# Y blocks loaded once into raw buffers, and the sums of the weight blocks spread over three conversion steps

## The chip, the cores and the metric

The kernel runs on one core of one Trainium2 chip. TensorE (PE) multiplies, VectorE (DVE), ScalarE (ACT) and GpSimd (POOL) do the elementwise work, and SyncE (SP) issues nearly all transfers. Each engine works through its own queue in order. The metric is device time in microseconds for one launch, the median of several runs.

## What is computed

Nystrom attention, its output as 2304 tokens of 512 features, and two MLPs behind each other. What the change touches lies in the second MLP.

```python
x = attn_out.transpose(0, 2, 1, 3).reshape(2304, 512)
h = x @ w_in            # 512 -> 2048
x = (h - np.tanh(h)) @ w_out
h = x @ w2_in           # second MLP
return (h * np.tanh(softplus(h))) @ w2_out
```

The matrices arrive as 64-bit floats, and are converted to 32-bit floats on the chip, from the two 32-bit halves of each number.

## The kernel before

**First MLP.** It runs in 128 slots (32 per batch entry, 16 per half of its tokens, one for each 128 hidden features). A slot multiplies (`h1`, L599 to L601), evicts and applies the function (`vec`: ACT, DVE, and POOL up to slot 103; L637 is DVE's last read of the product), and adds the product of three slots before into y (`y1`). At the end of 16 slots y goes through a raw buffer into DRAM (`ys`).

**Second MLP.** The tokens come in three blocks of 768 (`u`), the hidden features in eight blocks of 256 (`j`); one (u, j) is a group, `k` = 0 to 23. A group forms the first product of 2 x 2 blocks with seven multiplications of combinations of blocks instead of eight (`product(k, p)`, p = 0 to 6, L735 to L737): the left operand is one of seven sums of blocks of y (`Y[u, p]`), the right one of seven sums of blocks of the weights (`W2c[j]`). Each float operand is held as two parts, hi and lo, rounded and rest, so each multiplication is three matmuls. `combine` (L753 to L788) adds the seven products up in four tiles x: ACT evicts products 0, 1 and 3 (L766, L768, L776), DVE adds the others (L761), POOL makes two sums of x22 (L769 after product 1, L777 after product 3). The tile x12 that product 3 fills is read by L777 before DVE adds product 4 to it. `mish` applies the function. Between the products TensorE does the units of the second product of the group before (`o2_units`, L802 to L804): two after each of products 0 to 4, one after 5 and 6. The products take turns in two PSUM tiles (`ps_h`).

**Weights of the second MLP.** In the first block of tokens the weights are converted beside the products: 32 jobs, in the order of blocks j two of `w_in` (a, then b), two of `w_out`. One step of `convert` starts a job (ACT L131, and L135 or DVE L138), ends the one before (DVE L142, L148), fetches a raw block two jobs ahead, and calls what the job two steps back left to do. Steps lie in seven late slots (114 to 127) and in each group of the first block at p = 1, 2, 4 and 6. With a and b complete (p = 1) `w2i_job` forms the sums: at once two parts of W[0], the sums t and three differences by POOL (L181), and one step later (`sums`, p = 2) the remaining hi parts on ACT (L174) and lo parts on POOL (L177); two steps after that `keep` writes W to DRAM, from where the second and third block of tokens read it. a and t come from the pool `p2["st"]` with two buffers, b and the others from `st_p` with four, raw blocks from `raw_p` with four.

**y of the second MLP.** `y_prep(u)` makes the seven `Y[u, p]`. For each p it loads the one or two blocks of y it needs (`load`, L699: two transfers per block) into the pool `yf` with three buffers, one p ahead; adds them (L714: POOL for u = 0 and for p divisible by 3, else DVE); and at the next step splits the result into hi (ACT, L724) and lo (DVE, L725). Its steps for u = 0 lie in the slots of `yearly`, those for u = 1 and 2 in groups 6 to 8 and 14 to 16: one after product 6 of group 6, one after each product of group 7, the last after product 0 of group 8.

**Order.** Up to slot 115 a scheduler sets the order of the instructions on each engine by priorities; from slot 116 on the order written in the code stands. Outputs leave through raw buffers (`o_evict`), six per block of tokens.

Of the kernel before, what the change touches and what calls it, by code (L numbers as in the profile page):

```python
# [8 lines left out]
F32 = mybir.dt.float32  # L9
# [18 lines left out]
def kernel(  # L28
# [87 lines left out]
    def raw_f32():  # L116
        return f32(raw_p.tile([128, 512, 2], U32, tag="raw", name="raw").rearrange("p f t -> p (f t)"))
# [44 lines left out]
    def w2i_job(f):  # L162

        def done(y):
            if f % 2 == 0:
                rows[f] = y
                return ()
            j, a, b = f // 2, rows.pop(f - 1), y
            k1, k2 = slice(0, 256), slice(256, 512)
            W = W2c[j] = [P_p.tile([128, 4, 2, 256], F32R, tag="P", name="P") for q in range(2)]  # L170
            t = p2["st"].tile([128, 512], F32, tag="y", name="y")

            def hi(q, i, n, src):
                A.activation(out=W[q][:, i:i + n, 0, :], in_=src.rearrange("p (n c) -> p n c", n=n), func=ACTF.Copy)  # L174

            def lo(q, i, n, src, eng):
                eng.tensor_tensor(out=W[q][:, i:i + n, 1, :], in0=src.rearrange("p (n c) -> p n c", n=n),  # L177
                                  in1=f32(W[q][:, i:i + n, 0, :]), op=ALU.subtract)

            def add(out, x, y, op=ALU.add):  # L180
                G.tensor_tensor(out=out, in0=x, in1=y, op=op)  # L181

            hi(0, 2, 1, b[:, k2])
            hi(0, 3, 1, a[:, k1])
            add(t[:, k1], a[:, k1], b[:, k2])
            add(t[:, k2], b[:, k1], b[:, k2])
            lo(0, 2, 1, b[:, k2], G)
            lo(0, 3, 1, a[:, k1], G)
            add(b[:, k1], b[:, k1], a[:, k1], ALU.subtract)
            add(b[:, k2], a[:, k2], b[:, k2], ALU.subtract)  # L190
            add(a[:, k1], a[:, k1], a[:, k2])

            def sums():
                hi(0, 0, 2, t)
                lo(0, 0, 2, t, G)
                hi(1, 1, 2, b)
                lo(1, 1, 2, b, G)
                hi(1, 0, 1, a[:, k1])
                lo(1, 0, 1, a[:, k1], G)

            def keep():
                for q in range(2):
                    n = 4 - q
                    nc.sync.dma_start(out=w2s[j][q][:, 0:n, :], in_=f32(W[q][:, 0:n].rearrange("p n t c -> p n (t c)")))

            return (1, sums), (3, keep)
        return (w2i[f], done, None) + ((p2["st"],) if f % 2 == 0 else ())

    rows, W2c = {}, {}
# [451 lines left out]
    def y1(s, half):  # L661
        f = s % 16
        gg = sv[s]
        w = W1o[f]
        for d in (2 * half, 2 * half + 1) if s < NW else ():
            if f == 0:
                yps[d] = ps_y.tile([128, 512], F32, tag="y", name="y")[:, 0:HS]
            mm(yps[d], w[:, 0, 128 * d:128 * d + 128], gg, start=(f == 0), stop=(f == NF - 1))
        for d in (2 * half, 2 * half + 1) if s >= NW else ():
            if f == 0:  # L670
                yps[d] = ps_y.tile([128, 512], F32, tag="y", name="y")[:, 0:HS]
            c = slice(128 * d, 128 * d + 128)
            mm(yps[d], w[:, 0, c], gg[:, 0, :], start=(f == 0), stop=False)  # L673
            mm(yps[d], w[:, 1, c], gg[:, 0, :], start=False, stop=False)  # L674
        for d in (2 * half, 2 * half + 1) if s >= NW else ():
            c = slice(128 * d, 128 * d + 128)
            mm(yps[d], w[:, 0, c], gg[:, 1, :], start=False, stop=(f == NF - 1))  # L677
        if f == NF - 1:
            o = raw_f32()[:, 0:2 * HS].rearrange("p (d n) -> p d n", d=2)
            for d in range(2):  # L680
                A.activation(out=o[:, d], in_=yps[2 * half + d], func=ACTF.Copy)
            nc.sync.dma_start(out=ys[s // 16][:, 2 * half:2 * half + 2], in_=o)
# [8 lines left out]
    def y_prep(u):  # L691

        def load(kh, th):
            t = p2["yf"].tile([128, 2, C2], F32, tag="yf", name="yf")
            n0 = 0
            while n0 < C2:
                i, o = divmod((2 * u + th) * C2 + n0, HS)
# [2 lines left out]
                n0 += n  # L700
            return t

        def source(p):
            return [load(*x) for x in YB[p][:2]]

        src = {0: source(0)}
        yield 1
        for p in range(8):
            if p + 1 < 7:
                src[p + 1] = source(p + 1)  # L710
            if p < 7 and len(src[p]) > 1:
                t, t2 = src[p]
                eng = G if u == 0 or p % 3 == 0 else V
                eng.tensor_tensor(out=t, in0=t, in1=t2, op=YB[p][2])  # L714
                yield 0
            if p:
                t = src.pop(p - 1)[0]
                if p < 7:
                    y = p2["yk"].tile([128, 2, 2, C2], F32R, tag="yk", name="yk")
                    y = Y[u, p - 1] = [y[:, a] for a in range(2)]  # L720
# [86 lines left out]
                yield  # L807

    def o_evict(u, tt, on_vector):
        o = raw_f32()[:, 0:512]  # L810
        if on_vector:
            V.tensor_copy(out=o, in_=ops[u, tt])
        else:
# [126 lines left out]
    if True:  # L940
# [44 lines left out]
            n += 1  # L985
        gens = {}
        early = [NS - x for x in (14, 12, 10, 7, 5, 3, 1)]
        yearly = [NS - 25 + 3 * i for i in range(8)]

        def bg(s):  # L990
            b, i = s // 32, s % 32
# [100 lines left out]
```

## Time and profile before

| | |
|---|---|
| median of 3 runs | 916.29 us (915.23 to 916.86) |
| profiled execution, whole | 916.21 us |
| its span, first to last instruction | 914.4 us |
| TensorE busy | 818.4 us, 89% of the span |
| DVE, ACT, POOL busy | 581.8, 555.0, 326.3 us |
| granted TensorE clock, mean over the span | 0.948 of full speed |

Busy shares are averages over stages with different limits. The useful views are those of one stretch: what an engine waits for there, and the instructions in order of time. A row of the timeline gives start, duration, engine, line, operation, the tile written and those read, and in brackets how long the engine was idle before and what ended that. Rows of neighbours of the same kind are merged (x2, x3); their duration is that of all.

### The profile page before, as it was taken

Reading aid. Unit: us, or ns where it says so; the run is one execution under the profiler, and the core shown is the slowest. Engines: PE = TensorE matmul, PEld = TensorE weight load, DVE = VectorE, ACT = ScalarE, POOL = GpSimd, SP = SyncE. Lnnn points to the kernel's source line nnn. Section 1 sums busy time; section 2 is a strip of 40 time slices with the busy share of each in tenths; the row PEclk is TensorE's granted clock in tenths of the full one; section 3 lists DMA queues with packets and bytes.
Section 4 is the critical chain, followed back from the end, with each engine's and each line's share of the span. In section 5 each row is a group of like instructions: output and inputs, shape, how many; then the busy total and the mean of one; then the engine's idle time right before and its main releaser. Section 6 shows DMA issues by size and latency. Waiting matters only on the chain. (4 is left out here: it accounts for less than half of the span.)

```text
span 914.4 us, 15092 instructions
## 1 busy us (share of the span) xinstructions
PE 818.4 (89%) x5384; PEld 694.3 (76%) x5384; DVE 581.8 (64%) x1282; ACT 555.0 (61%) x1325; POOL 326.3 (36%) x349
## 2 busy tenths in 40 slices
PE   4799998999999999987868888875999995999998
PEld 2346786899889987887767777664898884899887
DVE  6688999987898778889765655543332334332332
ACT  5688976887788778777765555543433433433333
POOL 0010027865876577303255555522101021111110
PEclk8599999999999999998889998998999999899999
DMA  9899302404150012353436445285433455433311
GB/s 331 281 338 361 113 32 94 170 1 132 49 183 33 29 47 73 105 167 101 173 135 248 183 178 181 92 267 181 184 128 93 142 175 173 176 129 115 128 35 69
DMA packets 54573, 133.11 MB, mean 146 GB/s; under 512 B 10721, under 2 KB 27617, under 8 KB 51425
## 3 DMA queue, kind: packets, MB, share of 16 engines
q1 hardware_dynamic: 53344, 127.94, 41.2%
q0 software_dynamic: 1152, 4.19, 1.1%
q8 instruction: 42, 0.69, 0.3%
q14 instruction: 35, 0.28, 0.1%
HBM read 103.81 MB, written 28.31 MB: 144 GB/s over the span
## 5 line engine op out<-in xcount | busy, mean ns | idle before, releaser
L761 DVE TENSOR_TENSOR x<-x,h 128x384 f32<-128x384 f32 x144 | 76.7, 552 | 145.2 <-PE h L737 124.6
L735 PE MATMUL h<-yk,P 128*128 128x384 f32 x288 | 101.8, 354 | 40.5 <-ACT x L776 24.2
L673 PE MATMUL y<-gg,w 128*128 128x288 f32 x448 | 135.3, 316 | 3.0 <-ACT gg L97 2.0
L674 PE MATMUL y<-gg,w 128*128 128x288 f32 x448 | 126.7, 298 | 0.0
L747 ACT ACTIVATE gg<-x 128x384 fp32r<-128x384 f32 x96 | 50.3, 524 | 113.9 <-DVE x L761 113.9
L98 POOL TENSOR_TENSOR gg<-g,gg 128x288 fp32r<-128x288 f32 x80 | 70.3, 879 | 112.4 <-ACT gg L97 110.2
L673 PEld LDWEIGHTS y<-gg,w 128*128 128x128 f32 x448 | 86.0, 192 | 22.9 <-issue 12.6
L736 PE MATMUL h<-yk,P 128*128 128x384 f32 x288 | 99.8, 347 | 0.0
L737 PE MATMUL h<-yk,P 128*128 128x384 f32 x288 | 99.7, 346 | 0.0
L677 PE MATMUL y<-gg,w 128*128 128x288 f32 x448 | 98.0, 301 | 1.6 <-DVE gg L98 0.9
L769 POOL TENSOR_TENSOR x<-x 128x384 f32<-128x384 f32 x24 | 25.8, 1075 | 203.2 <-ACT x L768 203.2
L735 PEld LDWEIGHTS h<-yk,P 128*128 128x128 f32 x288 | 56.3, 196 | 51.9 <-ACT x L776 27.0
L674 PEld LDWEIGHTS y<-gg,w 128*128 128x128 f32 x448 | 86.0, 192 | 0.7
L630 POOL TENSOR_SCALAR mk<-s 128x288 uint8<-128x288 f32 x80 | 77.0, 963 | 10.5 <-ACT s L624 4.2
L651 DVE COPY_PREDICATED g<-mk,th 128x288 f32<-128x288 uint8 x128 | 76.9, 600 | 5.0 <-DVE g L647 0.5
L750 DVE TENSOR_TENSOR gg<-x,gg 128x384 fp32r<-128x384 f32 x96 | 54.2, 565 | 40.5 <-ACT x L748 40.5
L804 PE MATMUL y<-w,gg 128*128 128x512 f32 x192 | 75.6, 394 | 0.0
L802 PE MATMUL y<-w,gg 128*128 128x512 f32 x192 | 75.6, 394 | 0.0
L803 PE MATMUL y<-w,gg 128*128 128x512 f32 x192 | 75.5, 393 | 0.0
L677 PEld LDWEIGHTS y<-gg,w 128*128 128x128 f32 x448 | 72.5, 191 | 3.4 <-POOL gg L98 1.9
L640 ACT ACTIVATE q<-q,bias_c 128x288 f32<-128x288 f32 x128 | 68.7, 537 | 2.4
L599 PE MATMUL h<-AT,P 128*128 128x288 f32 x192 | 58.9, 307 | 12.4 <-DVE th L637 12.4
(161 smaller groups left out, 2077.9 us busy)
## 6 DMA issues: line engine op xcount, KB each, us to landing
P<-w2s SPq DMA_DIRECT2D x16, 1024.0 KB, 4.8
w<-w1s SPq DMA_DIRECT2D x24, 512.0 KB, 4.7
P<-w2s SPq DMA_DIRECT2D x16, 768.0 KB, 4.1
raw<-in_w1i_dram SPq DMA_DIRECT2D x16, 512.0 KB, 6.6
raw<-in_w1o_dram SPq DMA_DIRECT2D x16, 512.0 KB, 5.2
raw<-in_w2i_dram SPq DMA_DIRECT2D x16, 512.0 KB, 3.5
raw<-in_w2o_dram SPq DMA_DIRECT2D x16, 512.0 KB, 3.6
w2s<-P SPq DMA_DIRECT2D x8, 1024.0 KB, 3.9
```

Of the source, the lines that this page charges most:

```text
L630: eng.tensor_scalar(out=mk, in0=e, scalar1=FT, scalar2=None, op0=ALU.is_ge)
L651: V.copy_predicated(out=g0, mask=mk0, data=t0)
L673: mm(yps[d], w[:, 0, c], gg[:, 0, :], start=(f == 0), stop=False)
L674: mm(yps[d], w[:, 1, c], gg[:, 0, :], start=False, stop=False)
L677: mm(yps[d], w[:, 0, c], gg[:, 1, :], start=False, stop=(f == NF - 1))
L735: mm(t, w[:, p % 4, 0, c], y[a][:, 0], start=(a == 0), stop=False)
L736: mm(t, w[:, p % 4, 0, c], y[a][:, 1], start=False, stop=False)
L737: mm(t, w[:, p % 4, 1, c], y[a][:, 0], start=False, stop=(a == 1))
L761: V.tensor_tensor(out=xs[k, blk], in0=xs[k, blk], in1=t, op=op)
L802: mm(q, gg[:, 0, cs], w[:, 0, :], start=first, stop=False)
L803: mm(q, gg[:, 0, cs], w[:, 1, :], start=False, stop=False)
L804: mm(q, gg[:, 1, cs], w[:, 0, :], start=False, stop=last)
```

## The change

- `y_prep` loads each of the four blocks of y once per block of tokens, all at its first step, into the four raw buffers; sums go into `yf` tiles, and the blocks that are used as they are are split out of the raw buffers. Before, twelve loads per block of tokens went into `yf`.
- t is taken from the raw buffers. At the first step the two sums t and two lo parts remain; the three differences go into the next step (`sums`), between the hi and the lo part of t; the hi and lo parts that need the differences go into a third step (`rest`, p = 4); `keep` comes one step later.
- The steps of `y_prep(0)` move from slots 103, 106, ..., 124 to 102, 104, 105, 106, 108, 109, 110, 112.
- Outputs go through `st_p` tiles instead of raw buffers; the last outputs of the first MLP go through `yf` tiles.

```diff
-            t = p2["st"].tile([128, 512], F32, tag="y", name="y")
+            t = raw_f32()[:, 0:512]
...
-            add(b[:, k1], b[:, k1], a[:, k1], ALU.subtract)
-            add(b[:, k2], a[:, k2], b[:, k2], ALU.subtract)
-            add(a[:, k1], a[:, k1], a[:, k2])
 
             def sums():
                 hi(0, 0, 2, t)
+                add(b[:, k1], b[:, k1], a[:, k1], ALU.subtract)
+                add(b[:, k2], a[:, k2], b[:, k2], ALU.subtract)
+                add(a[:, k1], a[:, k1], a[:, k2])
                 lo(0, 0, 2, t, G)
+
+            def rest():
                 hi(1, 1, 2, b)
+                hi(1, 0, 1, a[:, k1])
                 lo(1, 1, 2, b, G)
-                hi(1, 0, 1, a[:, k1])
                 lo(1, 0, 1, a[:, k1], G)
...
-            return (1, sums), (3, keep)
+            return (1, sums), (2, rest), (4, keep)
...
-            o = raw_f32()[:, 0:2 * HS].rearrange("p (d n) -> p d n", d=2)
+            o = (raw_f32() if s < NS - 1 else p2["yf"].tile([128, 2, C2], F32, tag="yf", name="yf").rearrange(
+                "p a n -> p (a n)"))[:, 0:2 * HS].rearrange("p (d n) -> p d n", d=2)
...
         def load(kh, th):
-            t = p2["yf"].tile([128, 2, C2], F32, tag="yf", name="yf")
+            t = raw_f32()[:, 0:2 * C2].rearrange("p (a n) -> p a n", a=2)
...
-        src = {0: source(0)}
+        blk = {x: load(*x) for x in ((0, 0), (1, 1), (1, 0), (0, 1))}
+        src = {}
         yield 1
         for p in range(8):
-            if p + 1 < 7:
-                src[p + 1] = source(p + 1)
-            if p < 7 and len(src[p]) > 1:
-                t, t2 = src[p]
-                eng = G if u == 0 or p % 3 == 0 else V
-                eng.tensor_tensor(out=t, in0=t, in1=t2, op=YB[p][2])
-                yield 0
+            if p < 7:
+                src[p] = blk[YB[p][0]]
+                if len(YB[p]) > 1:
+                    t = src[p] = p2["yf"].tile([128, 2, C2], F32, tag="yf", name="yf")
+                    eng = G if u == 0 or p % 3 == 0 else V
+                    eng.tensor_tensor(out=t, in0=blk[YB[p][0]], in1=blk[YB[p][1]], op=YB[p][2])
+                    yield 0
...
-        o = raw_f32()[:, 0:512]
+        o = st_p.tile([128, 512], F32, tag="y", name="y")
...
-        yearly = [NS - 25 + 3 * i for i in range(8)]
+        yearly = [NS - 26] + [NS - 24 + i + i // 3 for i in range(7)]
```

Behind the edits the lines of the changed kernel are one or two higher (L776 becomes L777, L714 becomes L715).

How it moves instructions. First ACT in a group of the first block of tokens, from the eviction of product 1 on; before (P are the parts of W, y the tiles a, b and t, w the weights of the second product):

```order
L768 ACTIVATE x<-h 128x384
L131 ACTIVATE y<-raw 128x512
L174 ACTIVATE P<-y 128x256 x2
L174 ACTIVATE P<-y 128x2x256 x2
L174 ACTIVATE P<-y 128x256
L131 ACTIVATE y<-raw 128x512
L135 ACTIVATE raw<-raw 128x512
L97 ACTIVATE w<-y 128x512
L747 ACTIVATE gg<-x 128x384
L748 ACTIVATE x<-x 128x384
L776 ACTIVATE x<-h 128x384
```

and now:

```order
L769 ACTIVATE x<-h 128x384
L131 ACTIVATE y<-raw 128x512
L174 ACTIVATE P<-y 128x256 x2
L174 ACTIVATE P<-raw 128x2x256
L131 ACTIVATE y<-raw 128x512
L135 ACTIVATE raw<-raw 128x512
L97 ACTIVATE w<-y 128x512
L748 ACTIVATE gg<-x 128x384
L749 ACTIVATE x<-x 128x384
L777 ACTIVATE x<-h 128x384
L174 ACTIVATE P<-y 128x2x256
L174 ACTIVATE P<-y 128x256
```

Two of the five conversions L174 have moved behind the eviction of product 3. POOL in the same group, between its two sums of x22, before:

```order
L769 TENSOR_TENSOR x<-x 128x384
L181 TENSOR_TENSOR y<-y 128x256 x2
L177 TENSOR_TENSOR P<-y,P 128x256 x2
L181 TENSOR_TENSOR y<-y 128x256 x3
L177 TENSOR_TENSOR P<-y,P 128x2x256 x2
L177 TENSOR_TENSOR P<-y,P 128x256
L777 TENSOR_TENSOR x<-x 128x384
```

and now:

```order
L770 TENSOR_TENSOR x<-x 128x384
L181 TENSOR_TENSOR raw<-y 128x256 x2
L177 TENSOR_TENSOR P<-y,P 128x256 x2
L181 TENSOR_TENSOR y<-y 128x256 x3
L177 TENSOR_TENSOR P<-raw,P 128x2x256
L778 TENSOR_TENSOR x<-x 128x384
L177 TENSOR_TENSOR P<-y,P 128x2x256
L177 TENSOR_TENSOR P<-y,P 128x256
```

Two subtractions have moved behind the second sum of x22. SP around the y loads of the third block of tokens (yf_8638 and the like are the buffers, ys5 to ys7 pieces of y in DRAM), the first twelve rows of before; after them come fourteen more transfers of y:

```order
L699 DMA yf_8638<-ys5_100 128x2x192
L699 DMA yf_8638<-ys6_101 128x2x192
L699 DMA yf_8641<-ys6_101 128x2x96
L699 DMA yf_8641<-ys7_102 128x2x288
L699 DMA yf_8661<-ys5_100 128x2x192
L699 DMA yf_8661<-ys6_101 128x2x192
L215 DMA P_8681<-w2s0_0_79 128x2048
L215 DMA P_8682<-w2s0_1_80 128x1536
L699 DMA yf_8689<-ys5_100 128x2x192
L699 DMA yf_8689<-ys6_101 128x2x192
L699 DMA yf_8692<-ys5_100 128x2x192
L699 DMA yf_8692<-ys6_101 128x2x192
```

and all of them now:

```order
L702 DMA raw_8600<-ys5_100 128x2x192
L702 DMA raw_8600<-ys6_101 128x2x192
L702 DMA raw_8603<-ys6_101 128x2x96
L702 DMA raw_8603<-ys7_102 128x2x288
L702 DMA raw_8606<-ys5_100 128x2x192
L702 DMA raw_8606<-ys6_101 128x2x192
L702 DMA raw_8609<-ys6_101 128x2x96
L702 DMA raw_8609<-ys7_102 128x2x288
L217 DMA P_8647<-w2s0_0_79 128x2048
L217 DMA P_8648<-w2s0_1_80 128x1536
```

All eight transfers now stand ahead of the load of the next weights. Last, POOL about slot 103, the end of its work for the first MLP (gg the lo part of the function's result, mk the mask), before:

```order
L98 TENSOR_TENSOR gg<-g,gg 128x288
L630 TENSOR_SCALAR mk<-s 128x288
L714 TENSOR_TENSOR yf<-yf 128x768 x4
L181 TENSOR_TENSOR y<-y 128x256 x2
L177 TENSOR_TENSOR P<-y,P 128x256 x2
```

and now:

```order
L632 TENSOR_SCALAR mk<-s 128x288
L715 TENSOR_TENSOR yf<-raw 128x768 x3
L98 TENSOR_TENSOR gg<-g,gg 128x288
L632 TENSOR_SCALAR mk<-s 128x288
L715 TENSOR_TENSOR yf<-raw 128x768 x2
L181 TENSOR_TENSOR raw<-y 128x256 x2
```

Three additions of y have moved ahead of the last lo part and the last mask on POOL.

## Rows read from the trace of the kernel before

**Rows 1.** Stages: edges, length, busy time (instructions) of each engine, clock, DMA share, GB/s

```profile
371.30:405.90 34.60, 32.40 (x236) 31.24 (x235) 31.99 (x83) 27.48 (x76) 6.41 (x4) 1.00 0.41 118
405.90:451.40 45.50, 33.10 (x200) 31.93 (x199) 36.96 (x83) 31.62 (x78) 14.54 (x12) 0.85 0.50 162
451.40:474.60 23.20, 15.36 (x81) 14.59 (x80) 14.86 (x28) 14.97 (x32) 12.18 (x12) 0.85 0.20 64
474.60:601.30 126.70, 104.33 (x469) 90.49 (x469) 76.78 (x132) 71.48 (x144) 68.82 (x72) 0.92 0.53 194
601.30:651.10 49.80, 37.38 (x158) 32.09 (x157) 18.28 (x35) 18.57 (x39) 9.58 (x7) 0.87 0.58 183
651.10:744.70 93.60, 93.60 (x470) 84.39 (x469) 31.94 (x63) 35.46 (x69) 13.94 (x13) 1.00 0.43 147
744.70:793.00 48.30, 36.83 (x158) 31.57 (x157) 18.50 (x36) 18.69 (x39) 7.74 (x6) 0.89 0.48 154
```

**Rows 2.** TensorE's waits from 400 to 452: us, times, longest

```profile
PE h L599 <- DVE th L637: 12.4, 4, 4.3
```

**Rows 3.** TensorE's waits from 474 to 602

```profile
PE h L735 <- ACT x L776: 19.3, 6, 3.8
PE h L735 <- DVE x L761: 3.1, 3, 2.3
```

**Rows 4.** Timeline of TensorE in group 4: first matmul of products 0, 1, 5, 6

```profile
537.93 0.34 PE L735 MATMUL h<-yk,P 128*128 128x384 f32 x1
...
540.37 0.34 PE L735 MATMUL h<-yk,P 128*128 128x384 f32 x1
...
554.00 0.69 PE L735 MATMUL h<-yk,P 128*128 128x384 f32 x1 [3.79 <-ACT x L776]
...
557.37 0.52 PE L735 MATMUL h<-AT,P 128*128 128x384 f32 x1
```

**Rows 5.** Timeline of ACT in group 4

```profile
548.91 1.12 ACT L174 ACTIVATE P<-y 128x512 fp32r<-128x512 f32 x2 [3.08 <-POOL y L181]
550.86 0.67 ACT L131 ACTIVATE y<-raw 128x512 f32<-128x512 f32 x1 [0.83 <-POOL P L177]
...
553.48 0.47 ACT L776 ACTIVATE x<-h 128x384 f32<-128x384 f32 x1
```

**Rows 6.** Timeline of POOL in group 4

```profile
542.18 1.14 POOL L769 TENSOR_TENSOR x<-x 128x384 f32<-128x384 f32 x1 [8.15 <-ACT x L768]
...
547.43 2.15 POOL L181 TENSOR_TENSOR y<-y 128x256 f32<-128x256 f32 x3
549.54 3.21 POOL L177 TENSOR_TENSOR P<-y,P 128x512 fp32r<-128x512 f32 x3
554.03 1.01 POOL L777 TENSOR_TENSOR x<-x 128x384 f32<-128x384 f32 x1 [1.28 <-ACT x L776]
```

**Rows 7.** Timeline of DVE in group 4: its first addition of product 4

```profile
555.07 0.56 DVE L761 TENSOR_TENSOR x<-x,h 128x384 f32<-128x384 f32 x1 [0.90 <-POOL x L777]
```

**Rows 8.** POOL's groups by shape: busy us, mean ns, idle before

```profile
L177 POOL TENSOR_TENSOR P<-y,P 128x512 fp32r<-128x512 f32 x16 | 20.7, 1311 | 4.3 <-PE y L677 4.3
```

**Rows 9.** DMA issues by line: KB of each, median us from issue to landing

```profile
raw<-in_w2i_dram SPq DMA_DIRECT2D x16, 512.0 KB, 3.5
```

**Rows 10.** Waits of all engines from 601 to 652

```profile
POOL yf L714 <- DMA yf<-ys: 30.0, 3, 12.7
```

**Rows 11.** Instructions on the tiles yf: ns min/median/max, first and last start

```profile
L699 SPq DMA_DIRECT2D yf<-ys x72: 359/462/942, 368.2 to 771.8; - x72
...
L725 DVE TENSOR_TENSOR yk<-yf,yk x36: 544/553/1098, 377.2 to 772.7; 128x384 fp32r<-128x384 f32 x36
L714 POOL TENSOR_TENSOR yf<-yf x11: 1800/1849/2711, 374.8 to 775.7; 128x768 f32<-128x768 f32 x11
```

**Rows 12.** Timeline of POOL in slot 122: the three differences of the first weights

```profile
427.38 2.94 POOL L181 TENSOR_TENSOR y<-y 128x256 f32<-128x256 f32 x3
```

More of the change, by code (lines that the diff above doesn't have):

```diff
@@ L701, in load @@
             return t
-        def source(p):
-            return [load(*x) for x in YB[p][:2]]
-        src = {0: source(0)}
+        blk = {x: load(*x) for x in ((0, 0), (1, 1), (1, 0), (0, 1))}
+        src = {}
         yield 1
         for p in range(8):
-            if p + 1 < 7:
-                src[p + 1] = source(p + 1)
-            if p < 7 and len(src[p]) > 1:
-                t, t2 = src[p]
-                eng = G if u == 0 or p % 3 == 0 else V
-                eng.tensor_tensor(out=t, in0=t, in1=t2, op=YB[p][2])
-                yield 0
+            if p < 7:
[5 more added lines that the diff above has]
+                    yield 0
             if p:
-                t = src.pop(p - 1)[0]
+                t = src.pop(p - 1)
                 if p < 7:
```

## The prediction

> **What bounds the kernel now.** I read the stages first [rows 1]; their edges are starts of the first product matmul of a group. A group is one pass over seven products; groups 0 to 7 belong to the first block of tokens, 8 to 15 to the second, 16 to 23 to the third. From 651.1 to 744.7 six groups take 93.60 us and TensorE is busy for all of it, at a granted clock of 1.00: 15.6 us is what a group costs when nothing is late. Against that floor:
> - groups 1 to 6 (474.6 to 601.3) take 126.7 us instead of 93.6: 33.1 too much;
> - groups 7 and 8, and 15 and 16, where the next tokens' y is prepared, take 49.8 and 48.3 instead of 31.2 each: 18.6 and 17.1, together 35.7 too much, of which TensorE idles 12.4 and 11.5 (49.8 - 37.38, 48.3 - 36.83);
> - group 0 takes 23.2 with TensorE busy for 15.4;
> - the last slots of the first MLP (405.9 to 451.4) take 45.5, of which TensorE idles 12.4, the 12.4 that it waits for DVE's L637 [rows 2]. Its clock is 0.85 there, so 30% of 45.5, some 13.7 us, ran at 1.2 instead of 2.4 GHz, which could give back up to 6.8.
>
> So TensorE bounds everything, and what can be had is its waits and what the clock loses with them: about 33 + 36 + 8 + 19 = 96 us. The profiled execution took 916.21 us, beside a median of 916.29, so the sum is made on 916.2.
>
> **Groups 1 to 6: what the wait is.** TensorE waits 19.3 us for ACT's L776 and 3.1 for DVE's L761 [rows 3]; the other 10.7 of the 33.1, 1.8 per group, goes with the clock (0.92). In group 4 [rows 4] products start 2.43 us apart; the two that carry one unit of the second product instead of two start (15.6 - 5 x 2.43) / 2 = 1.73 before the next. Product 5, due at 550.2, starts at 554.00 after 3.79 us of idling, product 6 at 557.37. Products alternate between two PSUM tiles, so product 5 needs the eviction of product 3, ACT's L776. That runs only at 553.48, because ACT stood in front of it: 3.08 us for the sums, 1.12 for converting them, 0.83 for the last of POOL's subtractions (which frees the buffer of the next a) [rows 5]. POOL meanwhile worked without a gap from L769 at 542.18 to 552.75, and L777 followed at 554.03 [rows 6]. DVE's addition into x12 must follow L777 and starts at 555.07 [rows 7]; product 6 starts 2.3 us after that.
>
> The change cuts this knot in two places. On ACT two conversions of the sums (L174) go behind the eviction of product 3, and t leaves the pool of a, so that the next a doesn't wait. ACT then reaches the eviction 3.08 + 1.12 + 0.83 = 5.0 us earlier, at 548.5, where 549.7 would do: **product 5 stops waiting**. On POOL two of the three subtractions at 549.54 go behind L777; the first, 512 wide, stays and costs 1.31 [rows 8]. So L777 runs from 550.85 to 551.9, and 2.3 us later, at 554.2, comes product 6. It would be due at 550.2 + 1.73 = 551.9: **a wait of 2.3 us remains at product 6**, set by POOL. The group then takes 554.2 + 1.73 - 537.9 = 18.0 at full clock. Whether the clock falls after a wait of that size no row here decides, so I add half of what it costs now, 0.9: 18.9. Six groups: 113.4, **13 us saved**. Bounds: 25 if 1.4 us over the floor are left per group, 5 if the clock costs as much as now and POOL is a little slower (20.3).
>
> What is added: t occupies one of four raw buffers, so five tiles share four buffers in every four conversion steps, and the load of a weight block waits for DVE's last use of a raw block in the same step, not the one before. The tightest is the load for product 1: DVE frees its buffer about when product 6 starts, 554.2, and ACT wants it when it has evicted product 1 of the next group, as long after that product's start as L769 (542.18 - 540.37 = 1.8): 555.9 + 2.4 + 1.8 = 560.1. A raw load lands in 3.5 us [rows 9], with an issue of 0.46 [rows 11] 4.0: hidden by some 2 us. If that cover were gone, ACT would stand at L131 and the sums behind it. The store of the finished block goes one step later on SP, behind loads that have landed by then.
>
> **Groups 7, 8, 15, 16.** POOL's additions wait 30.0 us for y loads in the first pair [rows 10]. Each addition needs two loads, these need one of three yf buffers, and a buffer needs the conversion two steps back: load, add, convert, load, in series. ACT and DVE stand in order behind it, and the evictions of the products with them. After the change four loads, of two transfers each, go out together at the end of groups 6 and 14, into raw buffers that no conversion uses any more. Eight issues of 0.46 and a landing of 3.5 are some 7 us, half a group; the sums have buffers of their own, which wait for nothing that is late. What is left per block is five additions, of 1.85 on POOL, and 14 splits of 0.55 on DVE [rows 11] and as many on ACT, 7.7 us in two groups of 15.6, beside 18.28 that DVE is busy in 49.8 now with the same work: it fits. I leave 0.5 us per group over the floor: **33.5 us saved**. Bounds 35.7, and 25 if a wait like that at product 6 above stays in each group.
> Outputs pass through four st buffers instead of four raw ones, so nothing changes.
>
> **The first y block, the last slots, group 0.** Before, the eight steps of the first y are spread from slot 103 to 124, among the weight conversions, and their loads stand before raw loads on SP. Now they lie in slots 102 to 112, before the conversions start. Slots 113 to 127 lose three y steps (six splits, one addition), and the sums hold ACT there less, as above. The 12.4 of waits and the 6.8 of clock can shrink; but DVE is busy 36.96 of 45.5 and POOL's sums still run beside it. I take **10 saved**, bounds 3 and 15. In return slots 102 to 112 get six more splits on DVE, busy 31.99 of 34.6 there [rows 1], 6 x 0.55 = 3.3, less the waits of the old steps; and three additions of 1.85 stand on POOL ahead of the last split and mask that it makes for the first MLP, for which y1 waits. **2 lost**, between nothing and 5. In group 0 the same two subtractions leave POOL's chain, 3.21 - 1.31 = 1.9, and ACT's waits go: **3 saved**, 0 to 6.
>
> **Sum.** 916.2 - 13 - 33.5 - 10 + 2 - 3 = **858.7 us**.
>
> **Rivals.**
> 1. POOL becomes the bound of groups 0 to 6, since more of DVE's work falls beside its chain. For it: three additions take 2.94 us at 427.38, in slots where DVE has little rest [rows 12], against 2.15 at 547.43, a factor of 1.37. On the 9.7 us from the start of L769 to the new end of L777 this is 3.6 more, a group of 22.5, more than the 21.1 of now, so these groups give nothing. Against it: DVE is busy 76.78 of 126.7 in these groups, so it gains much room to keep away. Time: 916.2 - 33.5 - 10 + 2 = 874.7. The Trainium skill (SBUF — State Buffer, Who interferes with whom) states that VectorE and GpSimd take a shared pair of ports by an exclusive lock when a VectorE instruction with two SBUF inputs meets a GpSimd instruction that reads SBUF. By that rule this rival's 874.7 would hold; the stretched row agrees with it in direction.
> 2. The floor is reached nearly everywhere: POOL's chain runs short and product 6 waits under 1 us. 916.2 - 29 - 35 - 12 - 6 = 834.2.
> 3. The change doesn't do what it says in the second block: the raw buffers of the last conversions (one is t of the last block) come free late, the loads land in group 7, and only the third block gains. 916.2 - 17 - 13 - 8 - 3 = 875.2.
> 4. Slower: the fifth tile starves the conversions. If each load's flight of 4.0 us showed whole in each of four steps, a group would grow by 16. The gains above are 57.5, so the turn comes at 8.2 us per group in groups 0 to 6, half of that flight exposed. With three of four exposed, 7 x 12 - 57.5 = 26.5 over: 942.7. Against it stands the cover of 2 us above.
>
> **Chances.** Forecast 0.60 (845 to 872), rival 1 0.17, rival 2 0.13 (828 to 845), rival 3 0.06, rival 4 0.04. The range takes in the upper half of rival 2 and both cases near 875: 838 to 882. Faster by over 0.2% (1.8 us, about what a measurement of this kernel can tell from no change): 0.95. Rival 4 gives the rest with what the slots may lose: within 0.2% 0.02, slower 0.03.
>
> **What would show it.** Right: in groups 1 to 6 no wait of product 5 for the eviction of product 3, one wait of some 2 us at product 6 for DVE behind POOL's addition after product 3, groups of 18 to 19.5; groups 7, 8, 15, 16 under 17 each; no addition that waits for a y load. Wrong: a raw load named as what ACT or DVE waited for; POOL operations longer than in [rows 6]; TensorE idle near 370 us behind POOL's three additions; groups 7 and 15 still over 19.

## The result, and the profile after

The changed kernel takes **876.0 us** (median of 4 runs, 875.88 to 876.19) beside 916.58 (915.23 to 919.08): a ratio of 0.9554, 95% interval 0.9534 to 0.9575. That is 40 us less; it is 17 us above the forecast of 858.7 and inside its range of 838 to 882, but outside the 845 to 872 that the forecast gave to its own mechanism. The profiled execution took 876.04, its span is 874.2, and the working below stands on it.

The stages first, with edges at the same matmuls as in [rows 1]. Columns: edges, length, busy time and instructions of TensorE, its weight loads, DVE, ACT and POOL, then granted clock, DMA share and GB/s.

```profile
372.10:411.80 39.70, 33.70 (x236) 32.53 (x234) 38.22 (x90) 31.52 (x86) 10.41 (x7) 0.96 0.18 59
411.80:446.70 34.90, 29.02 (x199) 27.94 (x200) 31.75 (x78) 28.01 (x71) 9.12 (x10) 0.95 0.37 127
446.70:468.30 21.60, 13.80 (x79) 12.61 (x79) 15.21 (x28) 14.63 (x32) 12.45 (x12) 0.97 0.36 117
468.30:591.50 123.20, 104.76 (x470) 92.44 (x470) 87.84 (x131) 71.12 (x143) 73.56 (x73) 0.92 0.55 193
591.50:625.70 34.20, 32.55 (x158) 28.64 (x156) 22.06 (x36) 18.27 (x39) 8.25 (x6) 0.98 0.50 179
...
719.30:752.80 33.50, 31.84 (x158) 27.93 (x157) 22.04 (x36) 18.27 (x39) 8.26 (x6) 1.00 0.32 116
```

Set against [rows 1], the 40.2 us of span (914.4 to 874.2) divide like this. Counted by first matmuls, the first stage there holds slots 104 to 116 (the prediction's "slots 102 to 112" goes by the steps of y), the second slots 117 to 127.

| stage | before | after | change | forecast |
|---|---|---|---|---|
| until slot 104 | 371.3 | 372.1 | +0.8 | 0 |
| slots 104 to 116 | 34.6 | 39.7 | +5.1 | +2 |
| slots 117 to 127 | 45.5 | 34.9 | -10.6 | -10 |
| group 0 | 23.2 | 21.6 | -1.6 | -3 |
| groups 1 to 6 | 126.7 | 123.2 | **-3.5** | **-13** |
| groups 7 and 8 | 49.8 | 34.2 | -15.6 | -33.5 for |
| groups 15 and 16 | 48.3 | 33.5 | -14.8 | these four |

The other groups take 15.6 us each, as before. So 9.5 of the missing 17.3 are in groups 1 to 6, 3.1 in groups 7, 8, 15 and 16, 3.9 ahead of slot 117. One number in the row for groups 1 to 6 says where to look: DVE is busy 87.84 us with 131 instructions, where it was 76.78 with 132 [rows 1]. The same work takes 11 us longer.

TensorE's and DVE's waits in groups 1 to 6 (us in total, times, longest):

```profile
PE h L736 <- DVE x L762: 18.4, 6, 3.2
DVE x L762 <- POOL x L778: 17.1, 6, 2.9
```

The wait of product 5 for ACT [rows 3] is gone. The only one left stands at product 6, behind DVE's second step with product 4 (the subtraction from x11), which stands behind POOL's addition into x22. Group 4 again, first TensorE (the first matmul of products 0, 1 and 6, and a later one of product 6), then POOL, then DVE:

```profile
530.70 0.52 PE L736 MATMUL h<-yk,P 128*128 128x384 f32 x1
...
533.64 0.34 PE L736 MATMUL h<-yk,P 128*128 128x384 f32 x1
...
548.46 0.44 PE L736 MATMUL h<-AT,P 128*128 128x384 f32 x1 [3.23 <-DVE x L762]
...
549.29 0.52 PE L736 MATMUL h<-AT,P 128*128 128x384 f32 x1
```

```profile
535.46 1.02 POOL L770 TENSOR_TENSOR x<-x 128x384 f32<-128x384 f32 x1 [8.74 <-ACT x L769]
...
539.69 3.36 POOL L181 TENSOR_TENSOR y<-y 128x256 f32<-128x256 f32 x3
543.01 1.30 POOL L177 TENSOR_TENSOR P<-raw,P 128x512 fp32r<-128x512 f32 x1
544.28 1.01 POOL L778 TENSOR_TENSOR x<-x 128x384 f32<-128x384 f32 x1
545.24 2.15 POOL L177 TENSOR_TENSOR P<-y,P 128x512 fp32r<-128x512 f32 x2
```

```profile
545.32 0.56 DVE L762 TENSOR_TENSOR x<-x,h 128x384 f32<-128x384 f32 x1 [2.87 <-POOL x L778]
545.79 1.01 DVE L138 TENSOR_SCALAR raw<-raw 128x512 uint32<-128x512 uint32 x1
546.72 1.22 DVE L142 SCALAR_TENSOR_TENSOR raw<-y,raw 128x512 uint32<-128x512 uint32 x1
547.86 0.54 DVE L762 TENSOR_TENSOR x<-x,h 128x384 f32<-128x384 f32 x1
```

POOL goes through its queue without a gap from 535.46 to 545.29, 9.83 us (forecast 9.7), the moved subtractions stand behind L778 as meant, and product 6 starts 3.2 us after L778's end, where 2.3 was forecast. Between DVE's two L762 lie two conversion steps of 1.01 and 1.22 us, beside POOL's moved subtractions (545.24 to 547.39).

### The profile page after: what moved, and what is told of

Read it like the earlier page. It is cut to its first block, busy times and chain, and to the rows that moved or that the text cites. A ratio compares the mean times of both kernels' runs of the same rounds, so it can differ in the third digit from the quotient of the medians.

```text
span 874.2 us, 14964 instructions
## 1 busy us (share of the span) xinstructions
PE 804.3 (92%) x5384; PEld 684.2 (78%) x5384; DVE 600.9 (69%) x1282; ACT 551.8 (63%) x1325; POOL 329.6 (38%) x349
## 4 chain that ended last, share of the span: by engine, by line
PE 54%; DVE 15%; POOL 11%; issue 8%; ACT 7%; DMA 4%; SPq 0%; POOLq 0%; DVEq 0%; ACTq 0%
PE h L736 4%; PE h L738 4%; PE h L737 4%; PE y L675 4%; PE y L679 3%; PE y L676 3%; PE y L805 3%; PE y L804 3%; PE y L803 3%; PE h L599 3%; POOL P L177 3%; PE y L670 2%; PE m L291 2%; POOL y L181 2%; DVE g L653 2%
## 5 line engine op out<-in xcount | busy, mean ns | idle before, releaser
L762 DVE TENSOR_TENSOR x<-x,h 128x384 f32<-128x384 f32 x144 | 76.4, 550 | 153.2 <-PE h L738 131.2
L98 POOL TENSOR_TENSOR gg<-g,gg 128x288 fp32r<-128x288 f32 x80 | 70.6, 883 | 110.8 <-ACT gg L97 108.7
L770 POOL TENSOR_TENSOR x<-x 128x384 f32<-128x384 f32 x24 | 25.1, 1045 | 210.6 <-ACT x L769 210.6
L736 PE MATMUL h<-yk,P 128*128 128x384 f32 x288 | 99.4, 345 | 3.5 <-ACT x L777 1.7
L675 PEld LDWEIGHTS y<-gg,w 128*128 128x128 f32 x448 | 84.9, 190 | 21.6 <-issue 12.6
L737 PE MATMUL h<-yk,P 128*128 128x384 f32 x288 | 98.4, 342 | 0.0
L738 PE MATMUL h<-yk,P 128*128 128x384 f32 x288 | 97.9, 340 | 0.0
L676 PEld LDWEIGHTS y<-gg,w 128*128 128x128 f32 x448 | 85.2, 190 | 0.7
L751 DVE TENSOR_TENSOR gg<-x,gg 128x384 fp32r<-128x384 f32 x96 | 59.7, 622 | 36.3 <-ACT x L749 36.3
L632 POOL TENSOR_SCALAR mk<-s 128x288 uint8<-128x288 f32 x80 | 77.0, 962 | 10.5 <-ACT s L626 4.1
L653 DVE COPY_PREDICATED g<-mk,th 128x288 f32<-128x288 uint8 x128 | 76.0, 594 | 5.1 <-DVE g L649 0.5
L679 PEld LDWEIGHTS y<-gg,w 128*128 128x128 f32 x448 | 71.9, 189 | 6.7 <-POOL gg L98 6.2
L638 DVE TENSOR_TENSOR g<-h,s 128x288 f32<-128x288 f32 x128 | 57.0, 445 | 19.8 <-ACT th L627 19.3
L626 ACT ACTIVATE s<-h 128x288 f32<-128x288 f32 x128 | 51.8, 404 | 25.3 <-PE h L603 14.6
```

Of the source, the lines that this page charges most:

```text
L632: eng.tensor_scalar(out=mk, in0=e, scalar1=FT, scalar2=None, op0=ALU.is_ge)
L653: V.copy_predicated(out=g0, mask=mk0, data=t0)
L736: mm(t, w[:, p % 4, 0, c], y[a][:, 0], start=(a == 0), stop=False)
L737: mm(t, w[:, p % 4, 0, c], y[a][:, 1], start=False, stop=False)
L738: mm(t, w[:, p % 4, 1, c], y[a][:, 0], start=False, stop=(a == 1))
L762: V.tensor_tensor(out=xs[k, blk], in0=xs[k, blk], in1=t, op=op)
```

## Experiments

All times are medians, and the ratios are to runs of the kernel before on the same chip; "after" is the changed kernel. The experiments are in four sets (e1 to e4, e5 to e8, e9 to e11, e12), each on a chip of its own, on which the kernel before took 916.4 to 918.4; so a difference of 1 or 2 us between two sets, or to after, is read from the stages and not from the times. The stages of the kernels that the text comes back to:

| stage | before | after | y only | sums only | e11 | e12 |
|---|---|---|---|---|---|---|
| slots 104 to 116 | 34.6 | 39.7 | 40.0 | 34.6 | 37.7 | 40.0 |
| slots 117 to 127 | 45.5 | 34.9 | 34.8 | 47.5 | 34.6 | 35.3 |
| group 0 | 23.2 | 21.6 | 22.6 | 20.4 | 19.0 | 19.5 |
| groups 1 to 6 | 126.7 | 123.2 | 129.0 | 124.0 | 107.3 | 107.3 |
| groups 7 and 8 | 49.8 | 34.2 | 33.1 | 51.1 | 31.2 | 31.2 |
| groups 15 and 16 | 48.3 | 33.5 | 33.4 | 46.8 | 31.2 | 31.2 |

### The two halves apart

**y only** (e1): after, with the function w2i_job of before.

```diff
-            t = raw_f32()[:, 0:512]
+            t = p2["st"].tile([128, 512], F32, tag="y", name="y")
...
-            return (1, sums), (2, rest), (4, keep)
+            return (1, sums), (3, keep)
```

> Only the loading and order of y and the staging of outputs are new; the sums stand as before (t in the pool of a, five additions and subtractions in a row). Theory: the two halves of the change don't touch each other. Groups 7, 8, 15 and 16 then take the 67.7 us that they take with the whole change (98.1 before), groups 1 to 6 stay at 126 to 127 and group 0 at 23; the last slots gain at most 3 of their 5.5. Time 882 to 887. Rival: the second block's loads are served only because the sums are through earlier; then groups 7 and 8 stay above 42 and the time above 893.

884.16 us, ratio 0.9635 (0.9605 to 0.9664): the theory's time. But the last slots, 104 to 127, gain 5.3 of their 5.5, where at most 3 was expected. In slots 117 to 127 the gain is 10.7, as large as with the whole change: it comes from y alone, from its steps leaving those slots. And groups 1 to 6 lose 2.3.

**Sums only** (e2): before, with the function w2i_job of after.

> Only the sums are new (t in a raw buffer, subtractions and conversions spread over three steps); y is loaded twelve times as before. Theory: groups 1 to 6 take 123 us as with the whole change (126.7 before), with one wait of 3.2 at product 6; groups 7, 8, 15, 16 stay at 98; the last slots and group 0 give 3 to 6. Time 907 to 911. Rival: the sums in the last slots are worth nothing without y moved away; then 912 to 913.

914.23 us, ratio 0.9957 (0.994 to 0.9974): neither, and a smaller gain than the rival's too. The sums give 2.7 in groups 1 to 6 and 2.8 in group 0, and lose 2 in the last slots. Groups 1 to 6 of the one and the other:

```profile
470.50:599.50 129.00, 107.00 (x469) 93.07 (x470) 76.28 (x132) 71.68 (x144) 68.26 (x72) 0.89 0.51 187
```

```profile
476.40:600.40 124.00, 105.12 (x469) 92.85 (x470) 88.24 (x132) 71.83 (x145) 73.98 (x73) 0.91 0.56 199
```

DVE's extra time, 12 us here (88.24 against 76.28, 132 instructions both times), comes with the sums' new order, and POOL's 5.7 more as well. Before, POOL's work fell into stretches in which DVE stood still with everything else; spread over the group it lies beside DVE's.

### What holds product 6

**The moved subtractions one step later** (e3; at product 6 instead of product 4):

```diff
-            return (1, sums), (2, rest), (4, keep)
+            return (1, sums), (3, rest), (4, keep)
```

> The two subtractions that stand behind x22's addition on POOL (and the conversions that they follow) go one conversion step on, to product 6. Theory: beside them DVE's L138 and L142 took 1.01 and 1.22 us instead of 0.42 and 0.69; with them gone product 6 starts 2.3 us after DVE's addition into x12 and not 3.2, so its wait is 2.3, groups 1 to 5 fall from 20.8 to 19.1 (the length that group 6 has, whose wait is 2.32) to 19.9, time 867 to 871. Rival: DVE's steps there are slow for a reason of their own, the wait stays 3.2, time 876. Second rival: the subtractions now slow the steps behind product 6 and the next group by as much, 874 to 876.

871.39 us, ratio 0.9495 (0.9472 to 0.9517). DVE's steps behind L778 in group 4:

```profile
542.67 0.56 DVE L762 TENSOR_TENSOR x<-x,h 128x384 f32<-128x384 f32 x1 [2.82 <-POOL x L778]
543.14 0.42 DVE L138 TENSOR_SCALAR raw<-raw 128x512 uint32<-128x512 uint32 x1
543.48 0.69 DVE L142 SCALAR_TENSOR_TENSOR raw<-y,raw 128x512 uint32<-128x512 uint32 x1
544.08 0.55 DVE L762 TENSOR_TENSOR x<-x,h 128x384 f32<-128x384 f32 x1
```

L138 and L142 are back at 0.42 and 0.69, and what lies between the two L762 is 1.1 us shorter: the term of 0.9 is POOL's moved subtractions. But groups 1 to 6 fall only to 120.5, the time is just above the theory's 867 to 871, and in groups 1, 4 and 6 the wait is 3.2 to 3.3 all the same. There POOL's queue from L770 to L778 takes longer, in group 4 11.4 us (531.22 to 542.64): DVE's L142 beside L770 takes 1.50, so that b, which POOL's first sum reads, is there 1.4 us after L770.

**x11 first** (e4) at product 4, so that only one step of DVE follows POOL:

```diff
-            acc("12")
-            yield 0
             acc("11", ALU.subtract)
+            yield 0
+            acc("12")
```

> At product 4 DVE subtracts from x11 first, which waits for nothing on POOL, does the conversion's two steps, and adds into x12 last, behind POOL's addition into x22. Theory: what product 6 waits for is POOL's chain of 9.8 us and then 3.2 us of DVE's steps behind it; these steps now run while DVE waited (2.87 us), and product 6 starts 0.7 us after POOL's addition: wait of 0.8 to 1.2, no loss of clock to speak of, groups 1 to 6 at 16.5 to 17.5, time 850 to 857. Rival: the steps of DVE that move ahead run beside POOL's chain and stretch it by as much as they save; wait above 2.2, group above 19, time 866 to 872.

866.26 us, ratio 0.9438 (0.9417 to 0.9458): the rival's time. Product 6 waits 2.2 to 2.3 in groups 2 to 4 and 1.3 to 1.8 in 1, 5 and 6; product 0 waits too, 0.5 to 0.8 in five of the six. POOL takes 11.4 us in group 4 from L770 (530.16) to the end of L778, instead of 9.8; its L778, then DVE:

```profile
540.10 1.43 POOL L778 TENSOR_TENSOR x<-x 128x384 f32<-128x384 f32 x1
```

```profile
538.91 1.78 DVE L142 SCALAR_TENSOR_TENSOR raw<-y,raw 128x512 uint32<-128x512 uint32 x1
541.57 0.56 DVE L762 TENSOR_TENSOR x<-x,h 128x384 f32<-128x384 f32 x1 [0.88 <-POOL x L778]
```

DVE's steps move up beside POOL's queue, and both get slower (L778 1.01 to 1.43, L142 0.69 to 1.78), and POOL's first sum stands 0.68 us for b again, whose last step on DVE takes 1.40 beside L770.

**The two additions of product 4 back to back** (e9), x22 still on POOL:

```diff
             acc("12")
-            yield 0
             acc("11", ALU.subtract)
```

> At product 4 DVE makes its two additions back to back; the conversion's L138 and L142, which stood between them, follow. x22 stays on POOL. Theory: product 6 is released some 1.3 us after POOL's addition into x22 instead of 3.2, its wait falls from 3.2 to about 1.3 to 1.6, the size that groups 7 and 15 have, which took 17.5 to 18.3; groups 1 to 6 at 17.2 to 18.3, time 857 to 864. Rival: with products on time DVE's steps fall beside more of POOL's chain, which was 9.8 us with the whole change and 11.4 where x11 came first, and the wait stays above 2.2: groups above 19, time 866 to 871.

868.48 us, ratio 0.9452 (0.9421 to 0.9482): the rival's time, by another way than it said. The wait at product 6 is down to 1.2 to 2.1, but product 0 now waits too, 0.9 to 1.4 us for DVE's L762 of product 5, behind the conversion steps that were moved.

**x22's second addition on DVE** (e5), so that nothing of POOL stands in the products' path at product 6:

```diff
-            G.tensor_tensor(out=xs[k, "22"], in0=xs[k, "22"], in1=xs[k, "12"], op=ALU.add)
+            V.tensor_tensor(out=xs[k, "22"], in0=xs[k, "22"], in1=xs[k, "12"], op=ALU.add)
```

> The second addition into x22 (L778) is made by DVE, right behind the eviction of product 3, and no longer by POOL behind its nine sums and subtractions. Theory: POOL's queue of 9.8 to 11.4 us between x22's first and second step is what sets product 6 in groups 0 to 6; without it the product's path has only ACT and DVE, product 6 is on time (wait under 0.5), the clock stays, groups 1 to 6 take 15.6 to 16.5 and group 0 gives 3 to 4: time 843 to 851. Rival: DVE is the bound, stretched beside POOL wherever its steps lie; another wait takes the place at product 6 or 0, groups stay above 18, time above 860.

861.73 us, ratio 0.9407 (0.938 to 0.9435): 14 below after and above what the theory allowed. DVE in group 4:

```profile
536.90 0.56 DVE L762 TENSOR_TENSOR x<-x,h 128x384 f32<-128x384 f32 x1
537.37 0.86 DVE L138 TENSOR_SCALAR raw<-raw 128x512 uint32<-128x512 uint32 x1
538.15 1.75 DVE L142 SCALAR_TENSOR_TENSOR raw<-y,raw 128x512 uint32<-128x512 uint32 x1
539.83 0.54 DVE L762 TENSOR_TENSOR x<-x,h 128x384 f32<-128x384 f32 x1
```

DVE waits for nobody between these steps, and product 6 still waits 1.9 to 2.8 in groups 1 to 5: L138 and L142, beside POOL's L177, take 2.6 us. POOL's queue as such accounts for part of the wait, DVE's steps beside POOL for the rest.

### The first y and the additions of y

**The first y's additions on DVE** (e6):

```diff
-                    eng = G if u == 0 or p % 3 == 0 else V
+                    eng = V if u == 0 or p % 3 else G
```

> The five additions for the first y go from POOL to DVE. Theory: in slot 104 TensorE waited 4.0 us because three additions of together 6.04 us stood on POOL ahead of its last split; without them that slot falls from 7.1 to 2.4 to 3.5 us and slot 110 to 2.4, against which DVE gets five additions of about 1.0 each (twice the 128x384 of 0.55) where it has little rest: net 1 to 4 saved, time 872 to 875. Rival: DVE is what sets the slots from 102 to 112 and gives it all back: 875 to 878.

873.52 us, ratio 0.9536 (0.9508 to 0.9563): in the theory's range, though the interval overlaps that of after, so the gain is read from the slots. In after, POOL in slots 103 and 104:

```profile
370.44 6.04 POOL L715 TENSOR_TENSOR yf<-raw 128x768 f32<-128x768 f32 x3
376.43 1.10 POOL L98 TENSOR_TENSOR gg<-g,gg 128x288 fp32r<-128x288 f32 x1
```

TensorE waited 4.0 us for that L98, and slot 104 took 7.1. Without the additions it takes 3.2, but slots 107 and 109 grow to 4.0 to 4.2, and slots 104 to 116 fall only from 39.7 to 37.8, of which DVE is busy 36.69. The additions on POOL were the first limit there; TensorE's waits that are left stand behind DVE, or behind ACT where ACT waits for DVE.

**Both** edits, e5 and e6, in one kernel (e7):

> Both of the last two edits: x22's second addition and the first y's additions on DVE. They lie in different stages (groups 0 to 6, slots 102 to 112), so the gains should add up: theory 840 to 848. Rival: as for each of them alone, above 860.

859.60 us, ratio 0.9379 (0.9357 to 0.9402): between the two. It is e5's time less 2.1, close to the 1.9 that the slots gave in e6; the gains add up as far as that shows, and what is missing was missing in e5.

**All of y's additions** on DVE, on top of both (e8):

```diff
-                    eng = G if u == 0 or p % 3 == 0 else V
+                    eng = V
```

> As the last one, and the three additions of the second and third y that POOL makes go to DVE too. In groups 7 and 15 product 6 waits 1.55 us for a DVE step that is stretched beside POOL's addition of 2.17. Theory: that wait goes, each of the two groups falls by 1.5 to 2.5, time 3 to 5 below the last one. Rival: DVE with five additions of about 1.0 us and fourteen splits in these two groups becomes late itself: no gain or up to 3 lost.

857.57 us, ratio 0.9358 (0.9332 to 0.9383). Groups 7 and 15 fall from 17.15 each to 15.60, the floor: 3.1 in the trace, 2.0 between the medians, where 3 to 5 was expected. What they had over it was the wait of product 6 for DVE, behind a split that lay beside POOL's addition. In after, group 7:

```profile
605.41 1.94 DVE L726 TENSOR_TENSOR yk<-yf,yk 128x384 fp32r<-128x384 f32 x1
```

```profile
605.11 1.83 POOL L715 TENSOR_TENSOR yf<-raw 128x768 f32<-128x768 f32 x1 [1.43 <-DVE yk L726]
```

A split of 0.55 us takes 1.94 and ends 0.4 after POOL's addition.

### Together

**e10**: e8 with the two additions of product 4 back to back.

> The additions back to back, and x22's second addition and all additions of y on DVE (the last kernel of the earlier set with one edit more). There product 6 waited 1.9 to 2.8 for DVE's second addition, held up by L138 and L142 of together 2.6 us beside POOL's subtractions. Theory: with nothing of POOL and no conversion step between eviction and release, product 6 waits under 0.6, the clock stays, groups 1 to 6 take 15.6 to 16.5 in place of 18.7, group 0 gives 1 to 2: time 839 to 846. Rival: the stretched steps come due at the next place (product 0 or 5) and groups stay above 17.5: time above 850.

856.76 us, ratio 0.9325 (0.9293 to 0.9358): the rival. Product 6 waits under 0.4 in groups 1 to 5, and the wait comes back at product 0, with 1.9 to 2.9 us in each group, here in group 5:

```profile
542.86 0.53 PE L736 MATMUL h<-yk,P 128*128 128x384 f32 x1 [2.24 <-DVE x L762]
```

Product 0 needs DVE's addition of product 5, and that stands behind L142 (1.79) and L148 (1.11), which run beside POOL's subtractions.

**e11**: e10 with the moved subtractions one step later, as in e3.

> As the last one, with the two subtractions of the second tile one conversion step later. Theory: if product 6 is on time without that, it changes nothing, within 1 us of the last one. Rival: what stays of the waits comes from DVE beside these subtractions, then 2 to 6 us faster; or they now stretch DVE's steps ahead of product 0, 2 to 6 slower.

**849.28 us**, ratio 0.9246 (0.9218 to 0.9274): the first rival, and more. No wait of groups 1 to 6 is over 1.4 us, and the granted clock is 1.00:

```profile
462.90:570.20 107.30, 98.00 (x468) 83.14 (x469) 94.23 (x136) 68.07 (x142) 72.00 (x66) 1.00 0.63 220
```

That is 27 us below after and the fastest kernel here. Groups 1 to 5 still take 18.2 each and group 6 16.1, with DVE busy for 94.23 of the 107.3. That is more than in after (87.84): the stretching has not gone, but less of it stands in the products' path.

**e12**: e11 with the subtractions of the first y's splits on POOL.

```diff
-                    V.tensor_tensor(out=y[a][:, 1, :], in0=t[:, a], in1=f32(y[a][:, 0, :]), op=ALU.subtract)
+                    (V if u else G).tensor_tensor(out=y[a][:, 1, :], in0=t[:, a], in1=f32(y[a][:, 0, :]), op=ALU.subtract)
```

> As the last one, and of the first y's splits the subtractions (fourteen, all but two in slots 104 to 116) go from DVE to POOL; the additions stay on DVE. In these slots DVE was busy 36.54 of 37.70 us in the last kernel, 31.99 of 34.60 before. Theory: DVE's count is what these slots take; twelve subtractions of 0.55 less are 6.6, the slots fall by 2 to 3.1 to the 34.6 to 35.7 that they took before, time 845.5 to 847.5. Rival: each subtraction on POOL, over 1 us long, stretches the DVE steps beside it by about what DVE is spared, as POOL's additions did to DVE's L653 (0.49 to 1.96), and the slots take 37 or more: 848 to 852.

853.71 us, ratio 0.9298 (0.9252 to 0.9344): no gain, and 1.7 above even the rival's range. The intervals of e11 and e12 overlap, so that it is slower isn't shown by the times; what happened to DVE is. Slots 104 to 116 in e11 and then in e12:

```profile
371.60:409.30 37.70, 34.02 (x235) 31.32 (x234) 36.54 (x94) 31.90 (x86) 0.93 (x1) 1.00 0.19 62
```

```profile
372.40:412.40 40.00, 34.24 (x236) 31.39 (x235) 39.60 (x83) 31.15 (x85) 15.03 (x13) 1.00 0.12 39
```

DVE has 11 instructions less and is busy 3 us longer. Its groups by shape there (busy us, mean ns of one, idle before), e11 and then e12:

```profile
L98 DVE TENSOR_TENSOR gg<-g,gg 128x288 fp32r<-128x288 f32 x13 | 5.7, 442 | 0.0
...
L653 DVE COPY_PREDICATED g<-mk,th 128x288 f32<-128x288 uint8 x12 | 5.7, 477 | 0.0
L639 DVE TENSOR_TENSOR th<-h,th 128x288 f32<-128x288 f32 x13 | 5.7, 439 | 0.0
L649 DVE TENSOR_TENSOR g<-q,g 128x288 f32<-128x288 f32 x12 | 5.3, 439 | 0.0
```

```profile
L98 DVE TENSOR_TENSOR gg<-g,gg 128x288 fp32r<-128x288 f32 x13 | 9.1, 702 | 0.2 <-ACT gg L97 0.2
L653 DVE COPY_PREDICATED g<-mk,th 128x288 f32<-128x288 uint8 x12 | 7.4, 618 | 0.0
L649 DVE TENSOR_TENSOR g<-q,g 128x288 f32<-128x288 f32 x13 | 7.3, 565 | 0.0
...
L639 DVE TENSOR_TENSOR th<-h,th 128x288 f32<-128x288 f32 x13 | 5.8, 444 | 0.0
```

The steps that read two tiles of SBUF grow, L98 from 442 to 702 ns, L649 from 439 to 565, L653 from 477 to 618; L639, which reads h from PSUM, stays (439, 444). So does L762, which reads h as well, in every kernel here, at 0.54 to 0.56, beside POOL or not. The Trainium skill (SBUF — State Buffer, Who interferes with whom) states just this line: a DVE instruction with two SBUF inputs contends with a GpSimd instruction that reads SBUF, one with at most one (outside its 2-port modes) does not. These rows agree; a step with one input that grows all the same, L632 (290 to 363 ns in these slots), is taken up at the end of the next section.

## Why the prediction came out as it did

The time lies in the range by a sum whose terms were not all right, and with luck: the range was drawn up to 882 to take in rivals 1 and 3. Two of the five gains and losses, groups 1 to 6 and slots 104 to 116, came out beyond their own bounds, the slots by 0.1.

**Slots 117 to 127**: -10 forecast, -10.6 measured. The reason given was half of one: y only shows the whole gain, and the sums, which the prediction counted in, cost 2 in those slots when alone.

**Groups 7, 8, 15, 16**: -33.5 forecast (35.7 less four times 0.5 is 33.7), -30.4 measured. The mechanism held: no addition waits for a y load any more [rows 10], and DVE and ACT fit in. 0.5 us per group over the floor was too little for groups 7 and 15, which took 18.25 and 17.49 (under 17 was to show that the forecast was right), since DVE's splits were counted at 0.55 us each, also beside POOL's additions; e8 shows it by taking these away.

**Groups 1 to 6**: -13 forecast with 5 as the least, -3.5 measured, the step that failed. The path was forecast rightly: product 5 stops waiting, and one wait at product 6 stays, behind POOL's addition and DVE. Its size was not. Group 4 took 20.8 instead of the 18.0 at full clock of the forecast, and 2.8 us are found in four places:
- 0.1 in POOL's queue, 9.83 against 9.7: this term was right in sum, with the three L181 longer (3.36, in [rows 6] 2.15, a sign of being wrong that the prediction had named) and other steps shorter;
- 0.9 in DVE's way from POOL's addition to product 6, 3.2 against 2.3. The 2.3 was read from [rows 7], where POOL had finished everything else. The change itself put two subtractions of POOL beside those steps; e3 takes them away and finds 0.42 and 0.69 again;
- 0.5 between products 0 and 1 and 1.3 between product 6 and the next group (548.46 to 551.5), the clock. The prediction took half of what the clock cost before; it costs all of it, 0.92 as before. The matmuls after the wait of 3.23 take 0.52 us instead of 0.34, in group after group.

So **rival 1 was the nearest** in its mechanism: DVE and POOL in each other's way is what the runs show. That its time, 874.7, is only 1.3 off is in part luck: it gave groups 0 to 6 nothing, they gave 5.1, and slots 104 to 116 and groups 7, 8, 15 and 16 took that back. Rival 3's 875.2 is as near, without its mechanism. The place was another than rival 1 said: POOL's queue ahead of L778 was not stretched on the whole, DVE was. And the argument held against it, that DVE has room to keep away in these groups, was the wrong way round. DVE's order is fixed, it doesn't keep away, and the idle time that it had lay where everything waited for POOL. Three of DVE's lines in groups 1 to 6 (busy us, mean ns, idle before them), before and after:

```profile
L142 DVE SCALAR_TENSOR_TENSOR raw<-y,raw 128x512 uint32<-128x512 uint32 x23 | 17.8, 776 | 0.0
...
L98 DVE TENSOR_TENSOR w<-y,w 128x512 fp32r<-128x512 f32 x12 | 8.4, 700 | 31.8 <-ACT w L97 31.8
L138 DVE TENSOR_SCALAR raw<-raw 128x512 uint32<-128x512 uint32 x11 | 4.7, 424 | 0.0
```

```profile
L142 DVE SCALAR_TENSOR_TENSOR raw<-y,raw 128x512 uint32<-128x512 uint32 x23 | 21.9, 952 | 0.0
...
L98 DVE TENSOR_TENSOR w<-y,w 128x512 fp32r<-128x512 f32 x12 | 11.9, 991 | 0.0
L138 DVE TENSOR_SCALAR raw<-raw 128x512 uint32<-128x512 uint32 x11 | 7.6, 687 | 0.0
```

Before, DVE stood 31.8 us ahead of L98 behind ACT, which stood behind POOL's subtractions [rows 5]; POOL worked alone then. Spreading POOL's work took that idle time away and put the same steps beside POOL, L98 at 991 ns instead of 700. L142 gives 4.1 of the 11 us, L98 3.5, the splits of the function's result (L751) 3.1 and L138 2.9; L148 takes 2.2 less, and L762 is unchanged.

Removing POOL from the path (e5) left a wait at product 6 behind DVE's conversion steps; shortening the path (e4, e9) moved part of the wait to product 0, and both together (e10) nearly all of it. None of the single edits tried reached the floor of rival 2 in these groups; e11 gets to 107.3, against 93.6.

**Slots 104 to 116**: +2 forecast with 5 as the bound, +5.1 measured. The named mechanism came (TensorE idles 4.0 us behind three additions), but they were priced at 1.85 each, and 6.04 for three is 2.0. The larger miss is that DVE had little room there, busy 31.99 of 34.60 [rows 1] and now 38.22 of 39.70, so that its 7 instructions more and their stretching show. In e6 the additions leave POOL and 3.2 of the 5.1 stay.

**Group 0**: -3 forecast, -1.6 measured, with a wait of 4.3 us at product 6 of the same kind as in groups 1 to 6.

**Rivals 3 and 4** did not come: in groups 1 to 8 no wait of ACT or DVE names a raw or y load. In groups 1 to 6 SP waits 44.2 us for DVE's L148 and 41.1 for POOL's L177 before it issues raw loads, and these land in 4.4 us (3.5 before, [rows 9]); the cover holds.

That DVE's 11 us come from running beside POOL is shown by e2, e3 and e12, and by after's groups 1 to 6 instruction by instruction. With no POOL instruction beside them L98, L142 and L148 take at most 0.69 us, L751 0.56 and L138 0.42; beside one L142 takes 1.21 to 1.27, L98 1.19 to 1.26, L751 1.09 to 1.95, L138 1.00 to 1.01 and L148 0.69 to 0.77. L762 keeps 0.54 to 0.56 beside POOL too.

What stays open is why L138, with one input, is among them, and with it L632, the mask, also a TENSOR_SCALAR with one input. Who starts first matters for L138: in after it starts 0.55 us after a subtraction of POOL, takes 1.01 and ends 0.3 after that one; in e11, where it starts some 0.2 ahead of POOL's L770, it takes 0.42. Whether it runs in one of the 2-port modes, no run tests. Nor was it tried whether a still later place for POOL's sums would bring groups 1 to 6 to the floor.

## What to carry to other kernels

Before spreading work of one engine into the gaps, look at who was idle in those gaps: with POOL and DVE, a gap that POOL leaves is worth little if DVE's two-input steps run in it. Price a DVE step with two SBUF inputs, in a stretch where POOL has work, at its own length and up to that of the POOL instruction beside it (0.55 became 1.94 beside 1.83), and prefer to keep the two engines from alternating on the path that TensorE waits for. When a wait moves each time that it is removed, compare the busy time of an engine with its count of instructions between the kernels: the same count with more time points to the cause, whatever line the wait names. What it costs depends on where the stretched steps lie: e11, the fastest kernel, has DVE busier than after.

## What the runs showed of the hardware

- Work taken off DVE and given to POOL made DVE busier: 94 instructions in 36.54 us, then 83 in 39.60.
- A DVE instruction beside a long one of POOL can take several times its length: a split of 0.55 us took 1.94, and in after L653, at 0.48 in e11's slots, took 1.96 at the start of POOL's three additions:

```profile
370.77 1.96 DVE L653 COPY_PREDICATED g<-mk,th 128x288 f32<-128x288 uint8 x1
```

- It goes both ways: POOL's L778 takes 1.01 us in after, where DVE waits for it, and 1.43 in e4, where it starts 0.6 us before DVE's L142 ends, which itself takes 1.78.
